# Products scaled into token order, stores of 128 rows, and the last rows projected as 384 and 128 columns

## The chip, the core and the metric

The kernel runs on one core of a Trainium2 chip. A core has five engines that work side by side and wait for one another through semaphores: TensorE (PE, matrix multiplications into the accumulator memory PSUM), VectorE (DVE), ScalarE (ACT), GpSimd (POOL) and SyncE (SP, which here only issues transfers). Transfers between the chip's memory and the core's working memory SBUF run on 16 DMA engines; SyncE, ScalarE and GpSimd issue them. The metric is the device time in microseconds (us) of one execution; three executions of the kernel before gave 328.26, 328.57 and 329.42 us, with the median 328.57.

## What is computed

Attention over a sliding window of 64 tokens, followed by a SwiGLU block. There are 8 batches of 576 tokens, 8 heads of 64.

```python
def _attn_ref(q, k, v):
    B, H, S, D = q.shape
    window = 64
    scale = 1.0 / np.sqrt(D)
    scores = scale * np.matmul(q, k.transpose(0, 1, 3, 2))
    pos = np.arange(S)
    rel = pos[:, None] - pos[None, :]
    mask = (rel >= 0) & (rel < window)
    scores = np.where(mask, scores, -1000000000.0)
    ...
    return np.matmul(attn, v)

def _moe_ref(x, w_gate, w_val, w_out):
    g = x @ w_gate
    silu = g * (1.0 / (1.0 + np.exp(-g)))
    val = x @ w_val
    return silu * val @ w_out
```

`x` is the attention's result, 4608 tokens by 512; the gate and value matrices are 512 by 1536, the output matrix 1536 by 512.

## The kernel before

The 4608 tokens are handled in nine groups of 512 (`NT = 9`), numbered t = 0 to 8. A group is the first 512 tokens of one batch, except group 7 (`LAST`), which holds the remaining 64 tokens of all eight batches. The order of all instructions is written out by hand (`manual_schedule`), and each engine takes its own in that order.

**Column order.** The 512 tokens of a group lie along the free dimension of `qT`, `xT` and `hT`. For t = 1 to 8, the queries are loaded with 16 neighbouring tokens to a partition (32 partitions for a group), and a 32-by-32 transpose on VectorE (L198) brings them into `qT`. The columns therefore stand in 16 blocks of 32: column 32e + x holds token 16x + e of the group. (For t = 0, below `TURNED`, there are four blocks of 128.) Matmuls of the attention pick the columns of a range of tokens through `blocks`. The keys are brought into token order by another transpose (L208), whose output is written four elements apart.

**A stage.** For each t, `scores` (L261) computes the scores of two pairs of heads, ScalarE takes the exponential (L274), VectorE masks it (L277) and adds neighbours (L282); `sums` gives the inverse of the totals through logarithm and exponential on ScalarE (L304, L307), and `mix_all` multiplies by the values (L347) into four PSUM tiles. `scale` (L359) then multiplies each tile by the inverse totals and writes one of the four parts of `xT[t]`, in bf16. The attention of group t is interleaved with the projection of group t - 1: `project` multiplies 128 columns of `hT` by the output matrix (12 matmuls of 512 columns, L410), VectorE copies the result to a tile `os_` (L417), and the store follows. The last projection of group t - 1 stands between the mixing and the gate matmuls of group t. Then `gate_value` runs twelve times: four gate matmuls and four value matmuls (L401), each four reading the four parts of `xT[t]` in order, then Silu on ScalarE (L394) and the product into `hT` (L395).

**PSUM.** The tiles `o_ps` and the gate's `g_ps` share a pair of buffers (tag "g"), so the second gate tile of a stage waits until the last `o_ps` has been copied.

**Stores.** The 128 rows of a tile `os_` are 128 neighbouring columns of `hT`, that is four blocks e of 32 tokens, each with 16 tokens between neighbours. `project_end` therefore issues four stores of 32 rows (L429), from SyncE; in the group t = 8, every other one from ScalarE. For t = 0 one store of 128 rows does (L420). `os_` has four buffers. SyncE also issues the loads of `v_f` (L137) in the same queue, among the stores.

**The end.** The last 128 rows go through `project_last`: two halves of 256 columns, each with 12 matmuls (L446), a copy (L450) and four stores of 32 rows by 256 columns (L453), two from SyncE and two from ScalarE. The transfers that SyncE and ScalarE issue are counted on eight semaphores, taken in turn (0 to 7, then 0 again); a transfer first waits for the one before it on its semaphore. At the end of the program SyncE waits for all of them in order, 0 to 7, and then the engines meet at barriers (L717).

Of the kernel before, what the change touches and what calls it, by code (L numbers as in the profile page):

```python
# [8 lines left out]
P = 128  # L9
# [8 lines left out]
def kernel(  # L18
# [10 lines left out]
    nc = tc.nc  # L29
    S, D, H = 576, 64, 8  # L30
    NTOK, DFF, DM = 4608, 1536, 512
    NT = NTOK // 512
    TURNED = 1
    LAST = NT - 2

    ctx.enter_context(tc.manual_schedule())
    cst = ctx.enter_context(tc.tile_pool(name="cst", bufs=1))
# [11 lines left out]
    wo = cst.tile([P, 12, DM], BF16, name="wo")  # L49
# [12 lines left out]
    def batch(t):  # L62
        return t if t < LAST else t - 1

# [6 lines left out]
    staged, queries, weights, inverse, xT, hT = {}, {}, {}, {}, {}, {}  # L71
# [9 lines left out]
    def load_q(t):  # L81
# [3 lines left out]
        for a, c in quarters:  # L85
            p0 = 64 * a + 32 * c
            if t != LAST:
                nc.gpsimd.dma_start(  # L88
# [26 lines left out]
    def load_qk(t):  # L115
        q_s = load_q(t)
        if t == 1:
            staged[t] = q_s, None
            return
        if t == LAST:  # L120
            groups = [(b, S - P) for b in range(4)]
# [122 lines left out]
    def scores(t, w):  # L244
# [3 lines left out]
        for j in range(8):  # L248
            if t == LAST:
                k_j = kT[t % 2 if j < 4 else 2]  # L250
# [4 lines left out]
            for lo, hi, c, src, k0 in pieces:  # L255
                for h in range(2):
                    for x in range(2):
# [11 lines left out]
                        )  # L269
        n = 1024 if t == LAST else 960  # L270
        for h in range(2):
# [8 lines left out]
            both = epool.tile([P, 8, 64], BF16, name="both", tag="both")  # L280
            lo = 2 if t == LAST else 0
            nc.vector.tensor_add(both[:], E[:, 1:17:2], E[:, lo:lo + 15:2])  # L282
# [17 lines left out]
    def room(n):  # L300
        return fsb.tile([P, 2, 512], FP32, name="r", tag="r", bufs=4)[:, 0:n]
# [54 lines left out]
    def scale(t, u, o_ps):  # L356
        if u == 0:
            xT[t] = att.tile([P, 4, 512], BF16, name="xT", tag="xT")
        nc.vector.tensor_mul(xT[t][:, u, :], o_ps, inverse.pop((t, u)))  # L359

    def values_first(u, o_ps):
        mix_first(u, o_ps)
        scale(0, u, o_ps)

    def wide(name):
        return ps_a.tile([P, 2, 512], FP32, name=name, tag="a")
# [4 lines left out]
    def mix_all(t):  # L371
        tiles = wide("ao_ps"), wide("ao_ps")
        for w in range(2):
            mix(t, w, (tiles[w][:, 0], tiles[w][:, 1]))
        for u in range(4):
            scale(t, u, tiles[u // 2][:, u % 2])
# [38 lines left out]
    def project_end(t, s, o_ps, copy=nc.vector.tensor_copy):  # L415
        os_ = fsb.tile([P, 512], FP32, name="os_", tag="os_", bufs=4)
        copy(os_[:], o_ps[:])  # L417
        rows = out[S * batch(t):S * batch(t) + 512]
        if t < TURNED:
            nc.sync.dma_start(rows.rearrange("(r e) f -> e r f", e=4)[s], os_[:])  # L420
            return
        if t == LAST:
            rows = out.rearrange("(b s) f -> b s f", s=S)[:, 512:S]
            rows = rows.rearrange("b (r e) f -> e b r f", e=16)
        else:
            rows = rows.rearrange("(r e) f -> e r f", e=16)
        for i in range(4):
            eng = nc.scalar if t == NT - 1 and i % 2 else nc.sync
            eng.dma_start(rows[4 * s + i], os_[32 * i:32 * i + 32])  # L429

    def out_tile():
        return ps_f.tile([P, 512], FP32, name="o_ps", tag="g")

    def project(t, s):
        o_ps = out_tile()
        project_part(t, (s,), (o_ps,), range(12))
        project_end(t, s, o_ps)

    def project_last(t, s):
        rows = out[S * batch(t):S * batch(t) + 512].rearrange("(r e) f -> e r f", e=16)  # L440
        os_ = fsb.tile([P, 512], FP32, name="os_", tag="os_", bufs=4)
        tiles = out_tile(), out_tile()
        for x in range(2):
            f = slice(256 * x, 256 * x + 256)
            for c in range(12):
                nc.tensor.matmul(  # L446
                    tiles[x][:, 0:256], hT[t][:, c, P * s:P * s + P], wo[:, c, f],
                    start=(c == 0), stop=(c == 11),
                )
            nc.vector.tensor_copy(os_[:, f], tiles[x][:, 0:256])  # L450
            for i in range(4):
                eng = nc.scalar if i % 2 else nc.sync
                eng.dma_start(rows[4 * s + i][:, f], os_[32 * i:32 * i + 32, f])  # L453

    def set_exp():
        nc.scalar.preload_act_table_set("natural_log_exp_and_others")  # L456
# [27 lines left out]
    for a in range(2):  # L484
        tr = tri[64 * a:64 * a + 64]
        nc.gpsimd.affine_select(
            out=tr[:, 1 - a], in_=tr[:, 1 - a], compare_op=ALU.is_ge, fill=0.0,
# [3 lines left out]
            out=tr[:, a], in_=tr[:, a], compare_op=ALU.is_ge, fill=0.0,  # L491
# [78 lines left out]
    d_ps, r = wide("d_ps"), room(2)  # L570
# [33 lines left out]
    for m in range(12):  # L604
# [15 lines left out]
        if 5 <= m < 9:  # L620
            u = m - 5
            join(on_a, keys[:, u], raw_k[:, 2 * u:2 * u + 2])
        if 6 <= m < 10:
            u = m - 6
# [8 lines left out]
    tiles = [ps_f.tile([P, 512], FP32, name="o_ps", tag=x) for x in "gvgv"]  # L633
# [15 lines left out]
    for s in range(4):  # L649
        project_end(0, s, tiles[s], on_a if s < 2 else on_v)  # L650

    for t in range(1, NT):
        if t > 1:
            set_exp()
            scores(t, 0)
            project(t - 1, 0)
            if t == 2:
                stage_v(3)
            o_ps = out_tile()
            project_part(t - 1, (1,), (o_ps,), range(5))  # L660
            scores(t, 1)
            sums(t, 0)
            project_part(t - 1, (1,), (o_ps,), range(5, 12))
            project_end(t - 1, 1, o_ps)
            project(t - 1, 2)
            sums(t, 1)
            mix_all(t)
            project(t - 1, 3)
# [21 lines left out]
    for s in range(3):  # L690
        project(NT - 1, s)
    project_last(NT - 1, 3)

# [28 lines left out]
```

## Time and profile before

| | |
|---|---|
| median of three runs | 328.57 us (328.26 to 329.42) |
| the profiled execution: span from the first to the last instruction | 326.2 us, mean granted TensorE clock 0.999 |
| L395, VectorE, product into `hT`, 108 of 128x512 | 74.7 us, 693 ns each |
| L417, VectorE, copies of `o_ps`, one of 128x512 | 678 to 692 ns |
| L450, VectorE, copies of `o_ps`, two of 128x256 | 0.8 us, 424 ns each |
| L617, VectorE, bf16 copies of 128, 256, 512 contiguous elements | 195, 228, 294 ns |
| SyncE's and ScalarE's transfers (queues q1 and q10) | 16.26 and 1.05 MB |
| whole core, DMA | 40.84 MB, mean 125 GB/s |

The median of the runs lies 2.4 us above the span of the profiled execution. In a line of a group, the count stands behind the x, then come the busy time in us and the mean of one instruction in ns, and behind the second bar the engine's idle time just before them. A line of a timeline begins with start and length in us; matmuls of a group overlap, so their length is from the first start to the last end. Lines marked SPq, ACTq or DVEq are what the engine's own queue does: issuing transfers, and waiting. Line numbers are those of the kernel before.

### The profile page before, as it was taken

What the parts mean: (1) busy time and instruction counts of PE and PEld (TensorE: products, weight loads), DVE (VectorE), ACT (ScalarE), POOL (GpSimd) and SP (SyncE); (2) the same over time, 40 slices, a digit from 0 to 9 for tenths busy, and PEclk for the clock granted to TensorE, in tenths of its full rate; (3) what the DMA queues carried; (4) which work ended last, traced back from release to release, by engine and by line L of the source; (5) the groups of instructions that cost most, each with busy time, mean ns of one, the idle gap of its engine ahead of it and who ended that gap; (6) DMA issues with size and microseconds to landing.
All of it is one profiled execution on the core that took longest, in us unless ns stands there. A gap on an engine that the chain in (4) does not pass through costs nothing.

```text
span 326.2 us, 6959 instructions
## 1 busy us (share of the span) xinstructions
PE 315.9 (97%) x2700; PEld 150.7 (46%) x2743; DVE 220.2 (67%) x352; ACT 167.2 (51%) x239; POOL 142.8 (44%) x256
## 2 busy tenths in 40 slices
PE   8899999999999999999999999999999999999995
PEld 3444444444444444444444544454444544444443
DVE  5865755587766776887678766876697586773431
ACT  5855557337733683358336743565347633773300
POOL 5944545986085893586024989464200000000000
PEclk9999999999999999999999999999999999999999
DMA  7999999999789999959812999799401300020013
GB/s 253 200 202 202 206 146 215 170 146 143 164 160 206 138 151 205 192 81 214 175 38 29 169 173 92 53 191 195 97 2 34 99 0 2 16 83 32 2 33 98
DMA packets 82865, 40.84 MB, mean 125 GB/s; under 512 B 64272, under 2 KB 78352, under 8 KB 82832
## 3 DMA queue, kind: packets, MB, share of 16 engines
q0 software_dynamic: 50672, 23.08, 57.7%
q1 hardware_dynamic: 31136, 16.26, 19.3%
q10 hardware_dynamic: 1024, 1.05, 1.1%
q8 instruction: 21, 0.34, 0.4%
q14 instruction: 12, 0.10, 0.1%
HBM read 54.00 MB, written 9.44 MB: 194 GB/s over the span
## 4 chain that ended last, share of the span: by engine, by line
PE 86%; DMA 8%; POOL 3%; issue 1%; DVE 1%; SPq 0%; DVEq 0%; POOLq 0%
PE o_ps L410 28%; PE g_ps L401 26%; PE v_ps L401 25%; DMA wv<-in_moe_w_val_dram 4%; DMA q_s<-in_q_dram 3%; PE s_ps L261 3%; PE ao_ps L347 2%; PE d_ps L294 1%; DMA q_f<-in_q_dram 1%; POOL wg L172 1%; POOL wv L172 1%; PE o_ps L446 1%; POOL v L129 1%; POOL qk_b L517 0%; DVE qT L198 0%
## 5 line engine op out<-in xcount | busy, mean ns | idle before, releaser
L394 ACT ACTIVATE sg<-g_ps 128x512 f32<-128x512 f32 x108 | 64.4, 597 | 113.8 <-PE g_ps L401 85.1
L395 DVE TENSOR_TENSOR hT<-sg,v_ps 128x512 bf16<-128x512 f32 x108 | 74.7, 693 | 59.8 <-PE v_ps L401 49.2
L401 PE MATMUL g_ps<-xT,wg 128*128 128x512 bf16 x415 | 108.2, 379 | 0.9
L401 PE MATMUL v_ps<-xT,wv 128*128 128x512 bf16 x415 | 107.2, 379 | 0.1
L410 PE MATMUL o_ps<-wo,hT 128*128 128x512 bf16 x396 | 93.6, 380 | 1.5 <-issue 0.3
L108 POOL DMA_DIRECT2D k_s<-in_k_dram x112 | 60.6, 552 | 26.2 <-DMA q_s<-in_q_dram 15.3
L401 PEld LDWEIGHTS <-wv 128*128 128x128 bf16 x424 | 41.5, 98 | 50.1
L401 PEld LDWEIGHTS <-wg 128*128 128x128 bf16 x424 | 41.3, 98 | 49.5 <-issue 0.6
L410 PEld LDWEIGHTS <-hT 128*128 128x128 bf16 x420 | 39.1, 98 | 46.5 <-issue 1.8
L274 ACT ACTIVATE eb<-s_ps 128x960 bf16<-128x960 f32 (+1 forms) x32 | 29.5, 974 | 16.4 <-PE s_ps L261 16.3
L208 DVE STREAM_TRANSPOSE kT<-k_s 128x512 bf16<-128x512 bf16 x28 | 36.0, 1284 | 0.3 <-issue 0.3
L277 DVE TENSOR_TENSOR eb<-eb,mask 128x960 bf16<-128x960 bf16 (+1 forms) x32 | 21.1, 658 | 14.4 <-ACT eb L274 14.4
L359 DVE TENSOR_TENSOR xT<-ao_ps,r 128x512 bf16<-128x512 f32 x36 | 23.0, 684 | 6.5 <-PE ao_ps L347 4.8
L162 POOL CAST vb<-v_f 128x512 bf16<-128x512 f32 x20 | 11.4, 618 | 31.9 <-DMA v_f<-in_v_dram 22.1
L304 ACT ACTIVATE r<-d_ps 128x512 f32<-128x512 f32 (+1 forms) x33 | 20.8, 629 | 6.2 <-PE d_ps L294 5.9
L198 DVE STREAM_TRANSPOSE qT<-q_s 128x512 bf16<-128x512 bf16 x32 | 22.4, 702 | 0.8 <-DMA q_s<-in_q_dram 0.8
L307 ACT ACTIVATE r<-r 128x512 f32<-128x512 f32 (+1 forms) x33 | 22.0, 669 | 1.0
L88 POOL DMA_DIRECT2D q_s<-in_q_dram x28 | 15.2, 564 | 10.2 <-DVE qT L198 4.8
L137 POOL DMA_DIRECT2D vb<-in_v_dram x16 | 10.9, 710 | 8.7 <-DMA wo<-in_moe_w_out_dram 3.7
L282 DVE TENSOR_TENSOR both<-eb 128x512 bf16<-128x512 bf16 x32 | 13.6, 425 | 1.1
L456 ACT ACT_TABLE_LOAD x9 | 11.5, 1283 | 2.0 <-issue 1.9
L95 POOL DMA_DIRECT2D q_s<-in_q_dram x16 | 8.6, 629 | 7.4 <-DVE qT L198 7.4
(107 smaller groups left out, 185.2 us busy)
## 6 DMA issues: line engine op xcount, KB each, us to landing
q_s<-in_q_dram POOLq DMA_DIRECT2D x28, 248.0 KB, 6.0
k_s<-in_k_dram POOLq DMA_DIRECT2D x112, 56.0 KB, 4.8
v_f<-in_v_dram SPq DMA_DIRECT2D x40, 128.0 KB
wo<-in_moe_w_out_dram POOLq DMA_DIRECT2D x3, 512.0 KB, 12.3
q_f<-in_q_dram SPq DMA_DIRECT2D x4, 256.0 KB
vb<-in_v_dram POOLq DMA_DIRECT2D x16, 64.0 KB, 2.9
v<-in_v_dram POOLq DMA_DIRECT2D x16, 64.0 KB, 3.1
q_s<-in_q_dram POOLq DMA_DIRECT2D x16, 62.0 KB, 3.6
```

Source lines behind the costliest of these rows:

```text
L108: nc.gpsimd.dma_start(k_s[p0:p0 + 32, g, :, 0:w], k[b, a:H:2, s:s + P].rearrange("u (r e) d -> r u (e d)", e=4) [:, :, 32 * c:32 * c + w],)
L198: nc.vector.transpose(queries[t][:, u, :].rearrange("r (e x) -> r e x", e=16), staged[t][0][:, u].rearrange("r (e d) -> r e d", d=D)[:, :, ...
L208: nc.vector.transpose(dst[:, u, :].rearrange("r (g x e) -> r g e x", g=4, e=4), k_s[:, :, u].rearrange("r g (e d) -> r g e d", d=D)[:, :, ...
L274: nc.scalar.activation(flat, s_ps[h][:].rearrange("r a b -> r (a b)")[:, 0:n], AF.Exp, scale=0.125)
L277: nc.vector.tensor_mul(flat, flat, mask[:].rearrange("r j c e y -> r (j c e y)")[:, 0:n])
L304: nc.scalar.activation(r, d_ps, AF.Ln)
L307: nc.scalar.activation(r, r, AF.Exp, scale=-1.0)
L359: nc.vector.tensor_mul(xT[t][:, u, :], o_ps, inverse.pop((t, u)))
L394: nc.scalar.activation(sg[:], g_ps[:], AF.Silu)
L395: nc.vector.tensor_mul(hT[t][:, m, :], sg[:], v_ps[:])
L401: nc.tensor.matmul(ps[:], w[:, c, P * m:P * m + P], xT[t][:, c, :], start=(c == 0), stop=(c == 3),)
L410: nc.tensor.matmul(o_ps[:], hT[t][:, c, P * s:P * s + P], wo[:, c, :], start=(c == 0), stop=(c == 11),)
```

## The change

`scale` writes the products, for t = 1 to 8, not in the order of its inputs but in token order: the inputs are still read in blocks of 32, and of each block the 32 results are written 16 elements apart. The four parts of `xT` and everything behind them (`hT`, `os_`) are then in token order, and a tile `os_` holds 128 neighbouring tokens. A store takes all 128 rows; for `LAST`, two stores take 64 rows each; for five tiles named in `HALVED`, two stores take 64 rows each. All stores are issued from SyncE. `project_last` computes 384 columns and then 128, each with one copy and one store. With the number of stores that results, the last store is counted on semaphore 7.

```diff
+    HALVED = [(1, 0), (1, 1), (1, 2), (1, 3), (2, 0)]
...
     def scale(t, u, o_ps):
...
-        nc.vector.tensor_mul(xT[t][:, u, :], o_ps, inverse.pop((t, u)))
+        x, r = xT[t][:, u, :], inverse.pop((t, u))
+        if t < TURNED:
+            nc.vector.tensor_mul(x, o_ps, r)
+            return
+        nc.vector.tensor_mul(
+            x.rearrange("r (x e) -> r e x", e=16),
+            o_ps.rearrange("r (e x) -> r e x", e=16),
+            r.rearrange("r (e x) -> r e x", e=16),
+        )
...
         rows = out[S * batch(t):S * batch(t) + 512]
         if t < TURNED:
             nc.sync.dma_start(rows.rearrange("(r e) f -> e r f", e=4)[s], os_[:])
-            return
-        if t == LAST:
-            rows = out.rearrange("(b s) f -> b s f", s=S)[:, 512:S]
-            rows = rows.rearrange("b (r e) f -> e b r f", e=16)
+        elif t == LAST:
+            for i in range(2):
+                r0 = S * (2 * s + i) + 512
+                nc.sync.dma_start(out[r0:r0 + 64], os_[64 * i:64 * i + 64])
         else:
-            rows = rows.rearrange("(r e) f -> e r f", e=16)
-        for i in range(4):
-            eng = nc.scalar if t == NT - 1 and i % 2 else nc.sync
-            eng.dma_start(rows[4 * s + i], os_[32 * i:32 * i + 32])
+            n = 2 if (t, s) in HALVED else 1
+            for i in range(n):
+                r = slice(P // n * i, P // n * (i + 1))
+                nc.sync.dma_start(rows[P * s:P * s + P][r], os_[r])
...
     def project_last(t, s):
-        rows = out[S * batch(t):S * batch(t) + 512].rearrange("(r e) f -> e r f", e=16)
+        r0 = S * batch(t) + P * s
         os_ = fsb.tile([P, 512], FP32, name="os_", tag="os_", bufs=4)
-        tiles = out_tile(), out_tile()
-        for x in range(2):
-            f = slice(256 * x, 256 * x + 256)
+        for f0, f1 in ((0, 384), (384, 512)):
+            o_ps = out_tile()
             for c in range(12):
                 nc.tensor.matmul(
-                    tiles[x][:, 0:256], hT[t][:, c, P * s:P * s + P], wo[:, c, f],
+                    o_ps[:, 0:f1 - f0], hT[t][:, c, P * s:P * s + P], wo[:, c, f0:f1],
                     start=(c == 0), stop=(c == 11),
                 )
-            nc.vector.tensor_copy(os_[:, f], tiles[x][:, 0:256])
-            for i in range(4):
-                eng = nc.scalar if i % 2 else nc.sync
-                eng.dma_start(rows[4 * s + i][:, f], os_[32 * i:32 * i + 32, f])
+            nc.vector.tensor_copy(os_[:, f0:f1], o_ps[:, 0:f1 - f0])
+            nc.sync.dma_start(out[r0:r0 + P, f0:f1], os_[:, f0:f1])
```

## The prediction

> **What bounds the kernel now.** I read the busy shares first, then the chain of work that ended last, then one stage's timeline, then the tail.
>
> ```profile
> PE 315.9 (97%) x2700; PEld 150.7 (46%) x2743; DVE 220.2 (67%) x352; ACT 167.2 (51%) x239; POOL 142.8 (44%) x256
> ...
> PE 86%; DMA 8%; POOL 3%; issue 1%; DVE 1%; SPq 0%; DVEq 0%; POOLq 0%
> ```
>
> TensorE (PE) is busy for 97% of the 326.2 us span, and the chain runs through it for 86%. An edit on another engine pays in two ways only: it makes PE wait inside a stage, or it shortens the tail after PE's last matmul. The change touches one place of each kind.
>
> Inside a stage, here t = 3, the two columns are start and length in us:
>
> ```profile
> 117.34 0.69 DVE L417 COPY os__1728<-o_ps 128x512 f32<-128x512 f32 x1 [0.67 <-PE o_ps L410]
> 118.19 2.68 DVE L359 TENSOR_TENSOR xT<-ao_ps,r 128x512 bf16<-128x512 f32 x4 [0.16 <-PE ao_ps L347]
> 118.42 2.77 PE L410 MATMUL o_ps<-wo,hT 128*128 128x512 bf16 x11
> 121.02 1.03 PE L401 MATMUL g_ps<-xT,wg 128*128 128x512 bf16 x4
> 121.22 0.69 DVE L417 COPY os__1830<-o_ps 128x512 f32<-128x512 f32 x1 [0.35 <-PE o_ps L410]
> ```
>
> The four scalings of L359 run on VectorE (DVE) while PE has just one projection to do, and then the gate matmuls read the four parts of `xT` in order. The last scaling ends at 118.19 + 2.68 = 120.87. The fourth gate matmul starts 3 × 0.216 after 121.02, at 121.67. So the scalings are hidden, with about 0.8 us to spare.
>
> The tail (SPq and ACTq are the queues of SyncE and ScalarE):
>
> ```profile
> 319.51 2.78 PE L446 MATMUL o_ps<-wo,hT 128*128 128x256 bf16 x24
> ...
> 321.02 0.42 DVE L450 COPY os__4457<-o_ps 128x256 f32<-128x256 f32 x1 [0.62 <-PE o_ps L446]
> 321.47 2.09 SPq L453 DMA_DIRECT2D out_dram<-os__4457  x4
> 321.48 2.16 ACTq L453 DMA_DIRECT2D out_dram<-os__4457  x4
> 322.33 0.42 DVE L450 COPY os__4457<-o_ps 128x256 f32<-128x256 f32 x1 [0.89 <-PE o_ps L446]
> ```
>
> PE ends at 322.3, the last copy at 322.75, the last issue at 321.48 + 2.16 = 323.64. Then SyncE waits for the landings and walks its closing waits:
>
> ```profile
> SPq L717 <- DMA out_dram<-os__4457: 1.2, 1, 1.2
> ```
> ```profile
> L717 SPq EVENT_SEMAPHORE  x8: 28/28/28, 324.9 to 325.3; - x8
> L717 SPq DRAIN  x1: 13/13/13, 325.4 to 325.4; - x1
> ```
>
> Eight waits, one for each DMA semaphore in order 0 to 7, start from 324.88 to 325.32 by the trace's own times, 0.062 apart. The built program puts the last two stores on semaphores 1 (SyncE) and 0 (ScalarE), so the first wait is the one that blocks, and the other seven are paid behind it.
>
> **Part 1: the scaled product in token order (L359, t = 1 to 8).** The count stays: 32 multiplications of 512 elements, both inputs f32 and contiguous. New is the write: neighbours of the inner loop are 16 bf16, 32 bytes, apart. No row has this operation with such a write. The rows that bound it:
>
> ```profile
> L208 DVE STREAM_TRANSPOSE kT<-k_s 128x512 bf16<-128x512 bf16 x28 | 36.0, 1284 | 0.3 <-issue 0.3
> ...
> L359 DVE TENSOR_TENSOR xT<-ao_ps,r 128x512 bf16<-128x512 f32 x36 | 23.0, 684 | 6.5 <-PE ao_ps L347 4.8
> ...
> L198 DVE STREAM_TRANSPOSE qT<-q_s 128x512 bf16<-128x512 bf16 x32 | 22.4, 702 | 0.8 <-DMA q_s<-in_q_dram 0.8
> ```
> ```profile
> L189 DVE COPY kT<-tp 128x512 bf16<-128x512 bf16 x8 | 5.5, 682 | 0.6 <-PE tp L186 0.6
> ...
> L612 DVE COPY mask<-tri 64x64 bf16<-64x64 bf16 x4 | 0.7, 206 | 0.0
> ```
>
> Call the extra time of one multiplication x. The lower end is 0: L359 already moves one element at a time (684 ns, as the f32 copies of 512 do), and nothing in a scattered write can be quicker. The upper end is L208 against L198: the same transpose of the same size takes 1284 ns where its bf16 output is written 8 bytes apart, and 702 where it is contiguous, so x = 0.58. Between them stand the rows with scattered reads: L189 reads 256 bytes apart in 682 ns, the pace of a contiguous f32 copy, and L612 reads 32 bytes apart, 64 elements in 206 ns where L617 copies 128 contiguous ones in 195. [...]
>
> What x does: four scalings back to back take 3 × 0.60 + 0.69 = 2.49 (2.48 in the stages t = 1 and t = 7), so the last can end at 118.19 + 2.49 + 4x = 120.68 + 4x (the 2.68 of t = 3 has a wait for ScalarE before the last one, which longer scalings swallow). With 0.05 for the signal, PE waits once 4x passes 121.67 - 0.05 - 120.68 = 0.94, that is from x = 0.235. Stages 2 to 6 and 8 have the same margin (start of the scalings to fourth gate matmul 3.48). For t = 7 it is 257.77 - 0.05 - 256.65 = 1.07, for t = 1 53.89 - 0.05 - 53.56 = 0.28. At x = 0 this is 0. At x = 0.58 it is 6 × (2.32 - 0.94) + (2.32 - 1.07) + (2.32 - 0.28) = 11.6 us. Behind a stalled scaling on DVE stand the copy of L417 and the product of L395. The copy must end before the second gate tile (122.75, later by the stall itself), and L395 waits for PE until 123.0, so neither adds a second wait.
>
> [...]
>
> **Part 2: one store in place of four.** In the built programs stores fall from 136 to 46, all of them issued by SyncE. Before, each costs SyncE 0.31 to 0.43 us of issue; it now has fewer, the `v_f` loads (L137) queued behind them start earlier, and the wait on each old store of the same semaphore is shorter. Nothing on PE's path waits for that: the casts that need `v_f` run at 117.19 for a mix at about 151, so the cover is over 30 us; without it a stage would wait for their 2.3 us. The five tiles of HALVED add five stores to that same idle queue. The DMA waits in front of each copy of L417 shrink from two or three instructions of 0.05 to one or two, where DVE is idle by 0.35. All 0.
>
> **Part 3: 384 and 128 columns.** PE: 36 matmuls of 512 columns take 7.93, 0.42 ns a column; 12 × 0.161 + 12 × 0.054 = 2.58 against 24 × 0.107 = 2.57. Should the 98 ns weight loads not hide behind 54 ns matmuls, it adds up to 12 × 0.044 = 0.53; but the eight 128-column transposes of L186 take 0.62 together, about 0.057 each after 0.22 for the last, so I take 0. DVE: 692 ns for 512 and 424 for 256 columns give 1.05 ns a column plus 0.156. The 384 copy runs from about 321.66 to 322.22, the 128 copy from 322.33 for 0.29 to 322.62: 0.13 earlier than 322.75.
>
> **Part 4: the last stores.**
>
> ```profile
> L420 SPq DMA_DIRECT2D out_dram<-os__895 x1: 360/360/360, 53.2 to 53.2; - x1
> ```
>
> A store of 128 rows is issued in 0.36. SyncE issues the first at 322.25 to 322.61, passes a semaphore wait, and starts the second at about 322.69. Before, the last issue (ScalarE's) started at 323.20 and its landing let SyncE go at 324.88, 1.68 later. With the same lag the landing comes at 324.37, 0.51 earlier. But the second store follows 192 KB on the same queue: with data 0.8 after the issue, at 323.05, and 215 to 297 GB/s (the stretches from 321.4 to 322.2), those take until 323.7 to 323.95, and 64 KB more until 324.0 to 324.3, against 324.5 before: 0.2 to 0.5 earlier. I take 0.45. [...]
>
> The last store now is on semaphore 7, so seven of the waits pass while SyncE still waits for data: 7 × 0.062 = 0.44.
>
> **Sum.** 0 + 0 + 0 - 0.45 - 0.44 = -0.9 us: a span of 325.3 for 326.2. The median of the runs, 328.57, is 2.4 above the span; that part is untouched, so 327.7 us, 0.27% less. The own range of this case is 327.2 to 328.3.
>
> **Rivals.** (a) The scattered write halves DVE's pace, as in L208. For it: the only row with scattered bf16 writes. [...] It decides from x = 0.25 (32x - 7 outweighs 0.9), a multiplication of 0.93 us; at L208's x the time is 328.57 + 11.6 - 0.9 = 339.3. (b) A part of that price, x from 0.25 to 0.4, as from steps spent on each of the 16 rows of the pattern. For it: L208 has 16 rows too; against it: L189 has 128 rows and no such price. 32x - 7 is 1.0 to 5.8, giving 328.7 to 333.5. (c) The tail gives nothing, since one queue carries what two did and the last 64 KB wait behind 192 KB, or 12 short matmuls wait for weights: 0.44 - 0.53 leaves 328.6.
>
> **Chances.** Forecast 0.54, (a) 0.34, (b) 0.07, (c) 0.05. About 0.3% (1.0 us) is what a measurement of this kernel can tell from no change. The forecast's 0.9 stands close to that bound: 0.31 of it faster, 0.23 within. (a) is slower, (b) slower by 0.06 and within by 0.01, (c) within. Faster 0.31, within 0.23 + 0.01 + 0.05 = 0.29, slower 0.40. The range runs from the forecast's low end past (a), 327.0 to 340.5.
>
> **What would show it.** Right: L359 near 0.68 us, the gate matmuls still 0.2 us behind the projection, one EVENT_SEMAPHORE instead of eight behind the last landing, PE's end as before. Wrong: L359 above 0.93 us, a gap in front of the third and fourth gate matmul with DVE xT as its releaser, eight times over.

## The result, and the profile after

| | before | after |
|---|---|---|
| median of the runs | 328.39 us (328.12 to 329.42, 6 runs) | 385.38 us (383.97 to 387.63, 6 runs) |
| span of the profiled execution | 326.2 us | 383.0 us |
| mean granted TensorE clock | 0.999 | 0.947 |

The ratio is 1.174 (95% interval 1.171 to 1.177): the kernel became 57 us slower. The prediction was 327.7, with a range from 327.0 to 340.5.

The page of the kernel after, from its busy shares, its 40 slices, its chain and its groups:

```profile
PE 335.4 (88%) x2700; PEld 154.2 (40%) x2743; DVE 269.3 (70%) x352; ACT 167.2 (44%) x239; POOL 143.6 (37%) x256
...
PEclk9999996999699998999899969996999989998999
...
PE 67%; DVE 16%; DMA 7%; issue 4%; POOL 3%; SPq 1%; ACT 1%; DVEq 0%; POOLq 0%
...
L410 PE MATMUL g_ps<-xT,wg 128*128 128x512 bf16 x415 | 120.0, 400 | 39.7 <-DVE xT L364 38.9
...
L364 DVE TENSOR_TENSOR xT<-ao_ps,r 128x512 bf16<-128x512 f32 x32 | 70.4, 2470 | 5.1 <-PE ao_ps L348 4.8
```

The scaling is L364 now. One takes 2470 ns where it took 684, DVE's share of the chain rises from 1% to 16%, and the gate matmuls (L410 now) stand idle 39.7 us in front, 38.9 of them waiting for `xT`. PE's busy time also rises, by 19.5 us with the same 2700 matmuls, and the granted clock dips in eight of the 40 slices, as many as there are stages from t = 1 to 8. No such dips were there before (mean 0.999).

One stage of the kernel after, as a timeline:

```profile
134.12 8.81 DVE L364 TENSOR_TENSOR xT<-ao_ps,r 128x512 bf16<-128x512 f32 x4 [0.16 <-PE ao_ps L348]
...
134.35 2.76 PE L419 MATMUL o_ps<-wo,hT 128*128 128x512 bf16 x11
...
136.96 0.38 PE L410 MATMUL g_ps<-xT,wg 128*128 128x512 bf16 x1
138.70 0.38 PE L410 MATMUL g_ps<-xT,wg 128*128 128x512 bf16 x1 [1.37 <-DVE xT L364]
...
140.85 0.38 PE L410 MATMUL g_ps<-xT,wg 128*128 128x512 bf16 x1 [1.77 <-DVE xT L364]
...
142.99 0.59 PE L410 MATMUL g_ps<-xT,wg 128*128 128x512 bf16 x1 [1.77 <-DVE xT L364]
...
143.37 1.91 PE L410 MATMUL v_ps<-xT,wv 128*128 128x512 bf16 x4
```

Four scalings last 8.81 us in place of 2.49. The projection that covered them is as short as before (2.76), so each of the other three gate matmuls waits for its own part of `xT`, and PE does four matmuls in the 6.4 us from 136.96 to 143.37. The four value matmuls behind take 1.91, where the gate's four took 1.03 before. The reason stands in three windows of the same stage (start and end, length, then the busy time of PE, PEld, DVE, ACT and POOL with their counts, the granted clock, the DMA share and GB/s):

```profile
140.00:143.00 3.00, 0.38 (x2) 0.10 (x2) 3.00 (x3) 0.00 (x0) 3.00 (x6) 0.98 0.87 87
143.00:146.40 3.40, 3.40 (x9) 1.22 (x9) 1.14 (x2) 0.60 (x1) 1.20 (x3) 0.51 1.05 164
146.40:150.00 3.60, 3.60 (x18) 1.61 (x17) 2.31 (x3) 1.19 (x2) 0.00 (x0) 1.00 1.09 201
```

In the stage t = 1, whose first four gate matmuls start from 53.5 to 59.9, the clock is low already inside the gaps:

```profile
57.00:61.00 4.00, 1.64 (x4) 0.51 (x4) 3.99 (x4) 0.44 (x1) 4.00 (x8) 0.57 1.11 131
61.00:65.00 4.00, 4.00 (x12) 1.47 (x11) 0.69 (x1) 0.76 (x2) 4.00 (x7) 0.58 1.21 189
```

Back in the stage shown, in the 3.4 us that follow the gap, the granted clock is 0.51: 9 matmuls run there, against 18 in the next 3.6 us. In the whole trace 78 matmuls last over 500 ns, and 6 before. So the four matmuls spread over the 6.4 us did not keep the clock up: it was 0.98 in the window that ends at 143.00, 0.51 in the next, and 1.00 from 146.40 on.

The tail of the kernel after:

```profile
377.29 2.78 PE L454 MATMUL o_ps<-wo,hT 128*128 128x384 bf16 x24
...
379.44 0.96 DVE L458 COPY os__4373<-o_ps 128x384 f32<-128x384 f32 x2 [1.26 <-PE o_ps L454]
380.02 0.81 SPq L459 DMA_DIRECT2D out_dram<-os__4373  x2
```
```profile
L723 SPq DRAIN  x2: 7/7/7, 382.2 to 382.3; - x2
L723 SPq EVENT_SEMAPHORE  x1: 28/28/28, 382.1 to 382.1; - x1
```

The 24 narrow matmuls take 2.78 as before, and one closing wait stands where eight did. From the start of this projection to the end of the program it is 5.74 us, and it was 6.72. So the tail did what was forecast, while 58 us went into the stages.

### The profile page after: what moved, and what is told of

It is laid out like the page before. It is cut to its first block, busy times and chain, and to the rows that moved or that the text cites. A ratio compares the mean times of both kernels' runs of the same rounds, so it can differ in the third digit from the quotient of the medians.

```text
span 383.0 us, 6839 instructions
## 1 busy us (share of the span) xinstructions
PE 335.4 (88%) x2700; PEld 154.2 (40%) x2743; DVE 269.3 (70%) x352; ACT 167.2 (44%) x239; POOL 143.6 (37%) x256
## 4 chain that ended last, share of the span: by engine, by line
PE 67%; DVE 16%; DMA 7%; issue 4%; POOL 3%; SPq 1%; ACT 1%; DVEq 0%; POOLq 0%
PE v_ps L410 23%; PE g_ps L410 23%; PE o_ps L419 17%; DVE xT L364 15%; DMA wv<-in_moe_w_val_dram 3%; DMA q_s<-in_q_dram 3%; PE s_ps L262 2%; PE d_ps L295 1%; DMA q_f<-in_q_dram 1%; PE ao_ps L348 1%; POOL wg L173 1%; SPq L138 1%; POOL wv L173 1%; PE o_ps L454 1%; DMA v_f<-in_v_dram 1%
## 5 line engine op out<-in xcount | busy, mean ns | idle before, releaser
L410 PE MATMUL g_ps<-xT,wg 128*128 128x512 bf16 x415 | 120.0, 400 | 39.7 <-DVE xT L364 38.9
L410 PE MATMUL v_ps<-xT,wv 128*128 128x512 bf16 x415 | 114.7, 400 | 0.1
L410 PEld LDWEIGHTS <-wg 128*128 128x128 bf16 x424 | 42.9, 102 | 82.8 <-issue 39.0
L364 DVE TENSOR_TENSOR xT<-ao_ps,r 128x512 bf16<-128x512 f32 x32 | 70.4, 2470 | 5.1 <-PE ao_ps L348 4.8
L410 PEld LDWEIGHTS <-wv 128*128 128x128 bf16 x424 | 43.1, 102 | 70.9 <-issue 25.9
```

The costliest lines, as they stand in the source:

```text
L364: nc.vector.tensor_mul(x.rearrange("r (x e) -> r e x", e=16), o_ps.rearrange("r (e x) -> r e x", e=16), r.rearrange("r (e x) -> r e x", e=16),
L410: nc.tensor.matmul(ps[:], w[:, c, P * m:P * m + P], xT[t][:, c, :], start=(c == 0), stop=(c == 3),)
```

## The experiments

Eight kernels were run. The first three part the write of the scaling from the rest of the change.

**e1: the same permutation by the reads.** The kernel after, with the products written in order and both inputs read 128 bytes apart.

```diff
         nc.vector.tensor_mul(
-            x.rearrange("r (x e) -> r e x", e=16),
-            o_ps.rearrange("r (e x) -> r e x", e=16),
-            r.rearrange("r (e x) -> r e x", e=16),
+            x.rearrange("r (x e) -> r x e", e=16),
+            o_ps.rearrange("r (e x) -> r x e", e=16),
+            r.rearrange("r (e x) -> r x e", e=16),
         )
```

> The changed kernel, but the scaling walks its output in order and reads both f32 inputs (PSUM and SBUF) 128 bytes apart. Theory W (the price lies on scattered bf16 writes alone): a multiplication takes 0.68 to 0.75 us, PE never waits for xT, and the time is 327.0 to 328.0, about 0.9 below the kernel before. Rival R (scattered access to memory costs the same read or written): 2.4 us each, 385 us. Rival P (the pattern of 16 rows costs, whatever its direction): 2.4 us each too, since the pattern has 32 rows here.

Measured: 331.70 us (331.26 to 332.61, 5 runs), ratio 1.0106 (1.0088 to 1.0123), against 328.32 for the kernel before. The group of the scaling, in the view of groups by shape:

```profile
L364 DVE TENSOR_TENSOR xT<-ao_ps,r 128x512 bf16<-128x512 f32 x32 | 31.1, 1037 | 5.1 <-PE ao_ps L348 4.8 <-ACT r L305 0.4
```

The same values arrive in the same places and the price falls from 2470 to 1037 ns: it hangs on the side on which the elements are scattered. But scattered reads are not free here either, and PE still waits for `xT`, 2.8 us over 9 times, the longest 0.6 us:

```profile
PE g_ps L410 <- DVE xT L364: 2.8, 9, 0.6
```

So none of the three ideas in the expectation holds as it stands: W had 327.0 to 328.0 us, R and P had 385.

**e2: the scattered write alone.** The kernel before, with only the multiplication exchanged.

```diff
-        nc.vector.tensor_mul(xT[t][:, u, :], o_ps, inverse.pop((t, u)))
+        x, r = xT[t][:, u, :], inverse.pop((t, u))
+        if t < TURNED:
+            nc.vector.tensor_mul(x, o_ps, r)
+            return
+        nc.vector.tensor_mul(
+            x.rearrange("r (x e) -> r e x", e=16),
+            o_ps.rearrange("r (e x) -> r e x", e=16),
+            r.rearrange("r (e x) -> r e x", e=16),
+        )
```

> The kernel before with only the scattered write of the scaling; stores and the last projection as before, so that the rows of the output stand in another order than the reference's. If the whole loss is the scaling, as theory W says, 385 to 387 us with 2.47 us a multiplication. If the stores of 128 rows or their single queue had a share in it, clearly less than 385: 340 to 380.

Measured: 387.97 us (2 runs), ratio 1.181 (1.179 to 1.183).

```profile
L363 DVE TENSOR_TENSOR xT<-ao_ps,r 128x512 bf16<-128x512 f32 x32 | 70.4, 2475 | 5.1 <-PE ao_ps L347 4.8 <-ACT r L304 0.4
```

The write alone makes the whole loss. Of the 2.6 us by which this kernel is slower than the one after, the old tail explains 1.05 (6.79 us against 5.74). The rest can't be told from the spread of the kernel after, whose six runs go with the granted clock: 383.97 and 384.87 us at 0.955, 387.63 at 0.938. The two runs here had 0.942 and 0.943.

**e3: the change without the scattered write.**

```diff
-        nc.vector.tensor_mul(
-            x.rearrange("r (x e) -> r e x", e=16),
-            o_ps.rearrange("r (e x) -> r e x", e=16),
-            r.rearrange("r (e x) -> r e x", e=16),
-        )
+        nc.vector.tensor_mul(x, o_ps, r)
```

> The changed kernel with the scaling as it was before (written in order), so that the rows of the output stand in another order than the reference's: the stores, the 384 and 128 columns and the last semaphore alone. My prediction's terms for these give 327.7 us (0.9 below), PE as before. If the single queue or the narrow matmuls cost, 328.4 or more.

Measured: 327.33 us (327.03 to 328.35, 9 runs), ratio 0.9969 (0.9958 to 0.9980). The scaling is back at its price, and the tail is 5.74 us.

```profile
L364 DVE TENSOR_TENSOR xT<-ao_ps,r 128x512 bf16<-128x512 f32 x32 | 20.4, 685 | 5.7 <-PE ao_ps L348 4.6 <-ACT r L305 0.4
```

Stores, columns and the last semaphore are together worth 1.0 us. The interval of the ratio does not reach 1, but it ends close to it.

**e4: the prices of single instructions.** The kernel before, and behind its end three each of the multiplication with other operands, and of ScalarE's copy. The core of the edit (`cols(out_b, 16)` writes bf16 elements 32 bytes apart):

```diff
+    def rows(ap, e):
+        return ap.rearrange("r (e x) -> r e x", e=e)
+    def cols(ap, e):
+        return ap.rearrange("r (x e) -> r e x", e=e)
...
+    for _ in range(3):
+        mul(cols(out_b, 16), rows(src[:], 16), rows(fac, 16))
...
+    for _ in range(3):
+        mul(rows(out_b, 16), cols(src[:], 16), rows(fac, 16))
```

> The kernel before with a row of single instructions behind its end, three of each: the same multiplication (f32 from PSUM and SBUF to bf16) written 2, 4, 8, 16 and 32 elements apart, in runs of 2 and 4, to f32, and read scattered; and ScalarE copies. Theory L (the price goes by pieces of 16 bytes that are touched, about 4 steps each): 4 bytes apart 0.7 to 0.9 us, 8 bytes 1.2 to 1.4, 16 bytes and more 2.3 to 2.5, runs of two at 16 bytes 1.2 to 1.4, f32 16 bytes apart 2.3 to 2.5. Rival E (every bf16 write that doesn't follow its neighbour costs 4 steps, whatever the distance): 2.3 to 2.5 from 4 bytes on, f32 not slowed. Scattered reads 0.68 to 0.75 in both.

Groups of this kernel by shape, VectorE first; `src` is in PSUM, `r` and the outputs are in SBUF:

```profile
L719 DVE TENSOR_TENSOR wg<-src,r 128x512 bf16<-128x512 f32 x3 | 7.3, 2421 | 0.1
...
L721 DVE TENSOR_TENSOR wg<-src,r 128x512 bf16<-128x512 f32 x3 | 6.9, 2295 | 0.1
L717 DVE TENSOR_TENSOR wg<-src,r 128x512 bf16<-128x512 f32 x3 | 3.9, 1292 | 0.1
L737 DVE TENSOR_TENSOR r<-src,r 128x512 f32<-128x512 f32 x3 | 3.2, 1058 | 0.1
...
L745 DVE TENSOR_TENSOR wg<-src,r 128x512 bf16<-128x512 f32 x3 | 3.0, 1013 | 0.1
L743 DVE TENSOR_TENSOR wg<-src,r 128x512 bf16<-128x512 f32 x3 | 3.0, 1003 | 0.1
L715 DVE TENSOR_TENSOR wg<-src,r 128x512 bf16<-128x512 f32 x3 | 2.2, 726 | 0.1
L729 DVE TENSOR_TENSOR wg<-src,r 128x512 bf16<-128x512 f32 x3 | 2.1, 692 | 0.1
L725 DVE TENSOR_TENSOR wg<-src,r 128x512 bf16<-128x512 f32 x3 | 2.1, 692 | 0.1
...
L741 DVE TENSOR_TENSOR wg<-src,r 128x512 bf16<-128x512 f32 x3 | 2.1, 684 | 0.1
```
```profile
L749 ACT CAST wg<-src 128x512 bf16<-128x512 f32 x3 | 6.9, 2292 | 0.1
L747 ACT CAST wg<-src 128x512 bf16<-128x512 f32 x3 | 1.8, 585 | 74.6 <-DVE wg L745 74.5
L751 ACT CAST wg<-src 128x512 bf16<-128x512 f32 x3 | 1.8, 585 | 0.1
```

| what is scattered | line | ns |
|---|---|---|
| nothing, bf16 written in order | L713 | 692 |
| nothing, but all three operands walked in 16 blocks of 32 | L725 | 692 |
| bf16 written 4 / 8 / 16 / 32 / 64 bytes apart | L715, L717, L719, L721, L723 | 726 / 1292 / 2421 / 2295 / 2380 |
| pairs of bf16 written, 16 bytes from pair to pair | L729 | 692 |
| f32 written 8 / 16 / 64 bytes apart | L735, L737, L739 | 691 / 1058 / 1015 |
| input in PSUM read 64 bytes apart | L741 | 684 |
| f32 input in SBUF read 64 bytes apart | L743 | 1003 |
| both inputs read 128 bytes apart, as in e1 | L745 | 1013 |
| ScalarE: in order / written 32 bytes apart / PSUM read scattered | L747, L749, L751 | 585 / 2292 / 585 |

Neither theory of this expectation came out whole. Theory L has the lone bf16 about right at every distance, but pairs at a pitch of 16 bytes, which it has at 1.2 to 1.4 us, took 692 ns, and f32 16 bytes apart, which it has at 2.3 to 2.5, took 1058. Elements 4 and 8 bytes apart, which rival E has at full price, took 726 and 1292. Scattered reads, which both have at 0.68 to 0.75, took 1003 from SBUF. What the rows say: a lone bf16 written 16, 32 or 64 bytes apart makes the multiplication take 2421, 2295 and 2380 ns, 3.3 to 3.5 times the 692 in order and no more at 64 bytes than at 16; 8 bytes apart it takes 1292, 1.9 times. Pairs of bf16 at a pitch of 16 bytes take 692, and f32 8, 16 and 64 bytes apart 691, 1058 and 1015. ScalarE's copy loses as much at the one distance that was run there (2292 against 585), so the price belongs to the write and not to the multiplication. e1's 1037 is the price of its reads from SBUF: L745 has the same pattern and 1013, L743 scatters the input in SBUF alone and has 1003. Why a bf16 written 16 bytes apart costs more (2421) than an f32 (1058) was not settled. And L717's 1292 lies close to the 1284 of the transposes of L208, so the plain price of a write 8 bytes apart is enough to explain that row.

**e5: the gaps filled.** The kernel after, with seven matmuls of ones ahead of the second, third and fourth gate matmul of a stage, into a tile that is overwritten anyway. PE waits as long for `xT`, but does not idle.

```diff
+                if t > 0 and m == 0 and ps is pair[0] and c > 0:
+                    for _ in range(7):
+                        nc.tensor.matmul(pair[1][:], ones[:, 0:P], ones[:])
```

> The changed kernel with 7 matmuls of ones in front of the second, third and fourth gate matmul of t = 1 to 8 (they write the value tile, which its own first matmul then starts afresh), so that PE works through the gaps in which it waits for xT; the waits themselves stay. Theory C (some 18 of the 57 us are not waiting but the matmuls that run at half pace after each gap, because the granted clock fell while PE idled): the matmuls of 0.63 us are gone, PEclk shows no dips, and the time falls from 385 to about 367. Rival S (the slow matmuls have another cause, such as what VectorE does to SBUF, or weights that come late): 385 or more.

Measured: 372.11 us (371.68 to 373.61, 4 runs), ratio 1.134 (1.132 to 1.136), with a mean granted clock of 1.000. From its page and the timeline of the same stage:

```profile
PEclk9999999999999999999999999999999999999999
```
```profile
134.88 0.38 PE L413 MATMUL g_ps<-xT,wg 128*128 128x512 bf16 x1
...
136.63 0.38 PE L413 MATMUL g_ps<-xT,wg 128*128 128x512 bf16 x1
...
136.84 1.67 PE L412 MATMUL v_ps<-ones 128*128 128x512 bf16 x7
...
140.95 0.38 PE L413 MATMUL g_ps<-xT,wg 128*128 128x512 bf16 x1 [0.27 <-DVE xT L364]
...
141.17 1.02 PE L413 MATMUL v_ps<-xT,wv 128*128 128x512 bf16 x4
```

The scalings are as slow (2488 ns) and the fourth gate matmul still comes 6.1 us behind the first (140.95 against 134.88), but the value matmuls behind it are back at 1.02. So rival S falls: VectorE writes as before, and the slow matmuls are gone. With 168 more matmuls the kernel is 13.3 us faster than after (385.38 - 372.11): that is what the lowered clock cost. Theory C had put it at 18. What is left against e3, 372.11 - 327.33 = 44.8 us, is the waiting itself. (The idle time of 38.9 us in the page of the kernel after is less, because it counts only from the end of the matmul before, 0.38 us behind its start, while matmuls in a row start 0.216 apart.)

**e6: token order by reads from PSUM alone.** By e4 a scattered read of PSUM costs nothing (684 ns against 692 in order) and one of SBUF does (1003). So ScalarE's logarithm, which reads `d_ps` from PSUM, puts the denominators into token order, and the scaling then reads only `o_ps` scattered.

```diff
+    def log_turned(r, d_ps):
+        nc.scalar.activation(
+            r.rearrange("r (x e) -> r x e", e=16),
+            d_ps.rearrange("r (e x) -> r x e", e=16), AF.Ln,
+        )
...
-            x.rearrange("r (x e) -> r e x", e=16),
-            o_ps.rearrange("r (e x) -> r e x", e=16),
-            r.rearrange("r (e x) -> r e x", e=16),
+            x.rearrange("r (x e) -> r x e", e=16),
+            o_ps.rearrange("r (e x) -> r x e", e=16),
+            r.rearrange("r (x e) -> r x e", e=16),
```

> The changed kernel, but token order comes from scattered reads of PSUM alone: ScalarE's logarithm reads the totals scattered and writes the inverse in token order, and the scaling reads the product from PSUM scattered, the inverse in order, and writes in order. By the prices of the single instructions (684 ns and 585 ns, as unscattered) nothing is added: 327.0 to 327.8, the same as the changed kernel without the scattered write (327.3). If a scattered read of PSUM beside PE's writes costs, or the logarithm's 128x1024 form does, 328 to 331.

Measured: 327.30 us (327.0 to 328.37, 7 runs), ratio 0.9970 (0.9959 to 0.9981). Its groups by shape, and the stage:

```profile
L373 DVE TENSOR_TENSOR xT<-ao_ps,r 128x512 bf16<-128x512 f32 x32 | 20.4, 685 | 5.7 <-PE ao_ps L357 4.8 <-ACT r L308 0.4
```
```profile
L308 ACT ACTIVATE r<-d_ps 128x512 f32<-128x512 f32 x28 | 16.5, 590 | 4.7 <-PE d_ps L295 4.7
```
```profile
117.92 2.68 DVE L373 TENSOR_TENSOR xT<-ao_ps,r 128x512 bf16<-128x512 f32 x4 [0.16 <-PE ao_ps L357]
...
118.15 2.76 PE L428 MATMUL o_ps<-wo,hT 128*128 128x512 bf16 x11
...
120.75 1.03 PE L419 MATMUL g_ps<-xT,wg 128*128 128x512 bf16 x4
```

Scaling and logarithm cost what they cost in order, the four gate matmuls stand close behind the projection again, and the kernel computes all that the change meant to. It is faster than the kernel before by 1.0 us and than the one after by 58.

**e7 and e8: the parts of the tail.** e6 without the five halved stores, so that the last store is counted on semaphore 2, and e6 with 256 and 256 columns.

```diff
-    HALVED = [(1, 0), (1, 1), (1, 2), (1, 3), (2, 0)]
+    HALVED = []
```
```diff
-        for f0, f1 in ((0, 384), (384, 512)):
+        for f0, f1 in ((0, 256), (256, 512)):
```

> The kernel e6_order_by_psum_reads without the five halved stores, so that the last store is counted on semaphore 2 and five waits stand behind it: if these waits cost 0.062 each, 0.3 more than e6 (327.3 to 328.1) and five EVENT_SEMAPHORE of SPq behind the last landing; if five stores less on the queue matter more, the same or less than e6.

> The kernel e6_order_by_psum_reads with the last rows projected as 256 and 256 columns: by my terms the second copy ends 0.13 later, and the last store holds 128 KB in rows of 1 KB behind 128 KB that left 0.6 earlier, so 0.1 to 0.4 more than e6. If the 192 KB in front of the last store held it up, the same or less.

Measured: e7 328.12 us (327.45 to 330.04, 12 runs), ratio 0.9996 (0.9981 to 1.0010); e8 327.48 us (327.22 to 328.31, 7 runs), ratio 0.9975 (0.9965 to 0.9985). The closing waits of e7:

```profile
L732 SPq EVENT_SEMAPHORE  x6: 28/28/28, 324.3 to 324.6; - x6
```

Five waits now follow the one that blocks, 0.31 us by 0.062 each, and e7's tail is 0.39 longer than e6's (6.13 against 5.74). e8's is 0.13 longer (5.88). Both agree with the sizes that the prediction gave to these steps, but it is the trace of one execution each that speaks: the medians of e8 and e6 lie too close to tell apart, and those of e7 and e6 lie 0.82 apart, of which the tail explains half. The rest is not explained; e7's runs spread over 2.6 us.

## Why the prediction was wrong

**The step that failed is the price of one scaling, x, in part 1.** The prediction took x = 0 and bounded it by 0.58 from above. No run shows this 0 for a bf16 written 32 bytes apart: in the kernel after, x is 2470 - 684 = 1.79 us for one, and 6.32 us for four back to back (8.81 - 2.49), 1.58 each. Two errors lie in it. The first is the choice of the value: of the two rows the prediction took the one of the same operation with contiguous writes (684 ns), and put the price of the slow one, L208 (1284), down to its being a transpose. That was the author's assumption, with no row behind it, and e4 shows that it isn't needed: a plain multiplication that writes 8 bytes apart takes 1292. The second is the upper bound. L208 writes 8 bytes apart, the change 32, and e4 shows that the price rises again between them, from 1292 to 2295. A bound taken from a stride of 8 bytes did not bound one of 32. The rows L189 and L612, which were to speak against a price, scatter their reads, and e4 shows reads and writes to be priced apart (64 bytes apart, 684 and 1003 ns for reads of f32 from PSUM and from SBUF, 2380 for writes of bf16). Nor were these reads free when like is set beside like. L189 reads bf16 from PSUM in 682 ns, and a row of the kernel before that the prediction didn't weigh copies as many bf16 from the same kind of tile, in order, in 417:

```profile
L531 DVE COPY qT<-tp 128x512 bf16<-128x512 bf16 x3 | 1.3, 417 | 0.8 <-PE tp L186 0.8
```

L612's 206 ns for 64 elements stand against an estimated 178 for 64 contiguous ones (L617's 195, 228 and 294 for 128, 256 and 512 give 0.26 each).

**The way from x to the stall was right.** The prediction's terms, with 4x = 6.32 in place of 0, give 6 × (6.32 - 0.94) + (6.32 - 1.07) + (6.32 - 0.28) = 43.6 us. Measured, with the clock held up, 44.8 (e5 against e3). e1 tests the same terms at a small x: 1.037 - 0.684 = 0.353 gives 32 × 0.353 - 7 = 4.3, and e1 lies 4.4 above e3. So rival (a) named the mechanism and its place, its 32x - 7 holds at both x that were run, and only the price in it was wrong. Rival (b), steps spent on each of the 16 rows of the pattern, falls by L725 of e4, which walks these rows without scattering and takes 692; that e1's x lies in its range comes from reads of SBUF.

**A term was missing: PE's clock.** The prediction counted a stall as lost waiting and nothing else, and gave no reason for leaving the clock out. At its own largest x the scalings would have come an estimated 1.18 us apart (the 0.60 from one to the next, and 0.58). At 2.14 us apart (the starts of the gate matmuls at 138.70, 140.85 and 142.99) PE does four matmuls in 6.4 us in the stage shown, and then runs at 0.51 for 3.4 us. This is 13.3 of the 57 us (e5). The waits of e1, 0.6 us at most, left the clock at 0.999; where between these two it begins to fall was not measured.

**Part 2, stores at no cost: right.** e3 holds all of the change but the scattered write, and its gain of 1.0 is what the tail alone explains. **Part 3: right.** PE's narrow matmuls cost nothing (2.78 for both), and the last copy ends 3.11 behind the projection's start in place of 3.24, the 0.13 that was forecast; e8 undoes it and loses 0.13 in its trace. **Part 4: right in size.** The last issue starts 3.16 behind the projection's start, and was 3.69. SyncE is let go at 4.84 in place of 5.37: -0.53, against -0.45. The lag from issue to release is 1.68 both times, so the 192 KB ahead in the queue cost nothing that shows. The seven closing waits are gone, 0.44. Rival (c), a tail that gives nothing, falls by this.

**The sum.** 43.6 of waiting by the prediction's terms, 13.3 of slow clock and -1.0 in the tail make 55.9 of the 57.0 that were measured. The range missed because x lies at nearly three times its upper bound (1.58 against 0.58), and the clock came on top.

## What to carry to other kernels

A bound holds only for the pattern it was measured on: before a stride is priced at nothing, or by the row of a smaller one, look for what changes between them, and if no row has the pattern, leave the range open upward. Reorder on the side where it is free, here f32 reads from PSUM (684 and 685 ns, against 692 and 684 in order), and not by lone bf16 writes 8 bytes or more apart in SBUF (1292 to 2421). Stalls of TensorE can be paid twice, as here with 44.8 us of waiting and 13.3 more of a lowered clock (0.51 in the 3.4 us behind the gap of the stage shown).

## What the runs showed of the hardware that was not expected

- A multiplication of 512 elements on VectorE that writes lone bf16 16, 32 or 64 bytes apart in SBUF takes 2295 to 2421 ns against 692 in order, and a copy on ScalarE that writes them 32 bytes apart takes 2292 against 585. Pairs of bf16 at a pitch of 16 bytes cost nothing more (692).
- Scattered reads of f32 cost nothing more from PSUM (684, and 585 on ScalarE), and from SBUF about half as much again (1003 against 692).
- Four matmuls spread over 6.4 us did not keep TensorE's clock up: the 3.4 us after them ran at 0.51. Useless matmuls in the gaps made the kernel 13.3 us faster.
